# Issuing the V-cache transfers of a decode-attention kernel from the ACT queue instead of the SP queue

## The chip, the cores and the metric

The kernel runs on one core of a Trainium2 chip. The metric is device time in microseconds (us), taken from the profiled core; lower is better. The core has a TensorE (PE), a VectorE (DVE), a ScalarE (ACT), a GpSimd (POOL) and a SyncE (SP), each with its own instruction stream. Transfers from HBM to on-chip memory are run by 16 DMA engines. SP and ACT can each issue transfers; each has its own DMA ring (q1 and q10 in the profiles below), a list of transfers that the DMA engines work off.

All runs that are compared here are fast runs, and each experiment was timed beside the kernel before on the same chip. Repeats of a kernel agree within 0.3%.

## The reference, cut to what matters

Four layers of one-token attention, A, B, A, B. In each layer 32 heads read their own K and V cache.

```python
# per layer: x is one row of 640, 32 heads, 8192 cached positions, head size 192
q = layernorm(x) @ wq                       # 640 x 6144
scores = einsum("hd,hkd->hk", q, k_cache) * 192 ** -0.5
p = softmax(scores)
o = einsum("hk,hkd->hd", p, v_cache)
x = x + o.reshape(6144) @ wo                # 6144 x 640
```

One head's K, and one head's V, is 8192 x 192 in bf16: 3072 KB. The program reads 868 MB and computes little with it.

## The kernel before

VectorE computes the scores: it multiplies the K tile by q in place (6.56 us) and adds up along the head dimension in a tree. ACT makes the softmax weights, PE multiplies them with V. Three buffers hold K, three hold V. The kernel is written as one loop in which every engine appends to its own stream, so the place of a call in the loop sets the order within that engine's stream.

```python
def sp_k(h, Kt=Kt):
    i = counters["k"] % NKSLOT                  # 3 slots
    counters["k"] += 1
    SP.wait(T["kslot"][i])                      # the row maximum of head h-3 is done
    ...                                         # dma_start(kslot[i], K[h])
    return i, SP.op(f, sem=semK[i], inc=16)

def sp_v(h, Vt=Vt):
    i = counters["v"] % NVSLOT                  # 3 slots
    counters["v"] += 1
    SP.wait(T["vslot"][i])                      # PE is done with V of head h-3
    ...                                         # dma_start(vslot[i], V[h])
    return i, SP.op(f, sem=semV[i], inc=16)
...
# start of a layer (l > 0)
for npair in range(min(NWQSET, NPAIR)):
    ev_wq[npair] = sp_wq(npair)
need_k(0); need_k(1); need_v(0); need_k(2)
ev_wo[0] = sp_wo(0)
...
for h in range(HRUN):                           # 32 heads
    need_k(h); need_k(h + 1); ...; need_v(h)    # SP: K(h+1), then V(h)
    ...
    cur = stage_tree_a(h, ki, ev_k)             # DVE: multiply
    if h >= 1: stage_M(heads[h - 1])
    if h >= 2: stage_out_dve(heads[h - 2])
    stage_tree_a2(cur)
    if h >= 1: stage_softmax(heads[h - 1], ...) # ACT: softmax; PE: times V(h-1)
    stage_act_rows(cur)                         # ACT: 8 of the 64 score columns
    if h >= 2: stage_out(heads[h - 2])          # ACT and PE: output row times wo
    stage_tree_b(cur)                           # DVE: rest of the tree; ACT: copy of the maximum
... # the last head's softmax and output, then the next layer
```

SP does nothing but issue. It runs ahead of the loop until a buffer is not yet free. ACT issues nothing.

Of the kernel before, what the change touches and what calls it, by code (L numbers as in the profile page):

```python
# [115 lines left out]
def build(nc, A_x, A_k, A_v, A_wq, A_wo, B_x, B_k, B_v, B_wq, B_wo, out, dbg=None, cfg=None):  # L116
# [34 lines left out]
    with ExitStack() as ctx:  # L151
        def sb(name, shape, dt):
            return ctx.enter_context(nc.sbuf_tensor(name, shape, dt))
# [4 lines left out]
        def sem(name):  # L158
            return ctx.enter_context(nc.semaphore(name))

        kslot = [sb(f"kslot{i}", [128, JJ * DH], BF16) for i in range(NKSLOT)]
        vslot = [sb(f"vslot{i}", [128, JJ * DH], BF16) for i in range(NVSLOT)]
# [46 lines left out]
        semV = [sem(f"semV{i}") for i in range(NVSLOT)]  # L209
# [6 lines left out]
        SP = Stream("SP", None)  # L216
        PE = Stream("PE", pPE)
        DV = Stream("DVE", pDVE)
        AC = Stream("ACT", pACT)
# [33 lines left out]
        for i_ in range(2):  # L253
# [5 lines left out]
        T = dict(  # L259
            kslot=[None] * NKSLOT,  # L260
            vslot=[None] * NVSLOT,
            wq=[None] * 2,
            wo=[None] * 2,
            qb=[None, None],
            qslot=[None] * 8,
            sa=[None, None],
            ob=[None, None],
# [16 lines left out]
        for l in range(NL):  # L284
# [30 lines left out]
            def sp_v(h, Vt=Vt):  # L315
                i = counters["v"] % NVSLOT
                counters["v"] += 1
                SP.wait(T["vslot"][i])
                def f(s, i=i, h=h):
                    return s.dma_start(vslot[i][:, :], Vt[0, h].rearrange("(p j) d -> p (j d)", p=128))  # L320
                return i, SP.op(f, sem=semV[i], inc=16)

            ev_wq = [None] * NPAIR
            ev_wo = [None] * NG
# [8 lines left out]
            def need_v(h):  # L333
                if h >= H:
                    return
                if ("v", h) not in kv:
                    kv[("v", h)] = sp_v(h)
# [428 lines left out]
```

## Time and profile before

| | |
|---|---|
| time | 2074.65 us median of 2 runs (2075.35 to 2075.65 us in the medians of the later sets of 9) |
| K and V transfers | 256 of 3072 KB, one landing every 7.3 us |
| VectorE work per head | 13.7 us |
| VectorE waiting for K | 213 us, in 105 of 128 heads |

From the page of the kernel before: the mean busy share of the 16 DMA engines in 40 slices of the span (9 is 90% or more), what they moved in each slice, the DMA ring, the engines' shares of the chain of work that ended last, VectorE's multiply (count, busy us, mean ns, idle us just before it), and two of the DMA issues (size of one, median us from issue to landing).

```profile
DMA  9999999999999999999999999999999999999995
GB/s 395 430 425 428 422 422 427 426 430 419 423 426 425 427 422 424 426 426 428 418 423 426 423 429 424 422 427 426 426 410 425 425 423 424 423 423 425 426 427 254
...
q1 hardware_dynamic: 77700, 868.24, 99.3%
...
DMA 45%; issue 25%; DVE 24%; PE 4%; ACT 1%; SPq 1%; POOL 0%; POOLq 0%; DVEq 0%; ACTq 0%
...
L463 DVE TENSOR_TENSOR kslot<-kslot,q_sb 128x12288 bf16<-128x12288 bf16 x128 | 839.3, 6557 | 226.2 <-DMA kslot<-in_A_k_cache_dram 116.6
...
kslot<-in_A_k_cache_dram SPq DMA_DIRECT2D x64, 3072.0 KB, 32.6
vslot<-in_A_v_cache_dram SPq DMA_DIRECT2D x64, 3072.0 KB, 36.1
```

The DMA engines are busy throughout, on one ring, at 410 to 430 GB/s in all slices but the first and the last. Most of the chain of waits is DMA. VectorE works 13.7 us per head, a K and a V take 14.6 us, the weights 1.2 us more on average: DMA is the limit, by 2 us per head.

From the waits of the kernel before: who waited for what, us in total, times, longest.

```profile
DVE kslot L463 <- DMA kslot<-in_A_k_cache_dram: 116.6, 56, 8.2
DVE kslot L463 <- DMA kslot<-in_B_k_cache_dram: 96.6, 49, 6.8
...
PE OB L557 <- DMA vslot<-in_B_v_cache_dram: 4.4, 5, 0.9
```

VectorE waits for K. PE hardly waits for V: V is early, K is just in time.

From the timeline of SP: start, us, instruction. Each pair is K(h+1), then V(h).

```profile
906.95 2.21 SPq L312 DMA_DIRECT2D kslot<-in_B_k_cache_dram  x1
909.30 6.51 SPq L320 DMA_DIRECT2D vslot<-in_B_v_cache_dram  x1
921.56 0.33 SPq L312 DMA_DIRECT2D kslot<-in_B_k_cache_dram  x1
923.45 3.78 SPq L320 DMA_DIRECT2D vslot<-in_B_v_cache_dram  x1
```

K goes out as soon as VectorE has finished a head, V 2 us later. An issue takes 0.33 us, or several us when many transfers are queued (median 0.33 us with four in flight, 3.8 us with six). On this one ring what is issued first lands first. In layer 0 the landing records of the trace (when a transfer's completion was signalled) give:

```
transfer   issued   landed
K(31)      469.9    503.0
V(30)      475.2    510.3
V(31)      486.5    517.8
```

So when the last K of a layer lands, two V transfers are still to come. The stretch that follows is the only one in which VectorE stands still for long: it finishes the last head (13.7 us), then waits 22 to 23 us for the softmax, the output product, the layer norm and the next q. The windows view for that stretch, from the landing of K(31) to the end of head 0 of the next layer (the last two numbers are the DMA share and GB/s):

```profile
core 0: us, PE busy (x) PEld busy (x) DVE busy (x) ACT busy (x) POOL busy (x), PEclk, DMA share, GB/s
503.00:553.50 50.50, 23.60 (x186) 16.65 (x184) 31.59 (x29) 12.05 (x60) 0.54 (x1) 0.71 1.00 417
```

DMA stays busy through it: V(30), V(31), the weights and the first K and V of the next layer are queued.

### The profile page before, as it was taken

What the parts mean: (1) busy time and instruction counts of PE and PEld (TensorE: products, weight loads), DVE (VectorE), ACT (ScalarE), POOL (GpSimd) and SP (SyncE); (2) the same over time, 40 slices, a digit from 0 to 9 for tenths busy, and PEclk for the clock granted to TensorE, in tenths of its full rate; (3) what the DMA queues carried; (4) which work ended last, traced back from release to release, by engine and by line L of the source; (5) the groups of instructions that cost most, each with busy time, mean ns of one, the idle gap of its engine ahead of it and who ended that gap; (6) DMA issues with size and microseconds to landing.
All of it is one profiled execution on the core that took longest, in us unless ns stands there. A gap on an engine that the chain in (4) does not pass through costs nothing.

```text
span 2073.2 us, 24389 instructions
## 1 busy us (share of the span) xinstructions
PE 1158.3 (56%) x9625; PEld 915.1 (44%) x9668; DVE 1764.8 (85%) x1190; ACT 596.1 (29%) x3254; POOL 3.1 (0%) x13
## 2 busy tenths in 40 slices
PE   2565556555465555566536565556563665556656
PEld 1444444444354444444425454445452454444444
DVE  7888888988698888898779888889878988888896
ACT  2222232232232322232223332223222332223232
POOL 0000000000000000000000000000000000000000
PEclk7777777877678777777767777777776777777877
DMA  9999999999999999999999999999999999999995
GB/s 395 430 425 428 422 422 427 426 430 419 423 426 425 427 422 424 426 426 428 418 423 426 423 429 424 422 427 426 426 410 425 425 423 424 423 423 425 426 427 254
DMA packets 77813, 869.79 MB, mean 420 GB/s; under 512 B 4994, under 2 KB 29572, under 8 KB 44932
## 3 DMA queue, kind: packets, MB, share of 16 engines
q1 hardware_dynamic: 77700, 868.24, 99.3%
q8 instruction: 76, 1.25, 0.2%
q14 instruction: 37, 0.30, 0.0%
HBM read 868.22 MB, written 0.00 MB: 419 GB/s over the span
## 4 chain that ended last, share of the span: by engine, by line
DMA 45%; issue 25%; DVE 24%; PE 4%; ACT 1%; SPq 1%; POOL 0%; POOLq 0%; DVEq 0%; ACTq 0%
DMA kslot<-in_B_k_cache_dram 28%; DMA kslot<-in_A_k_cache_dram 17%; DVE kslot L463 12%; DVE kslot L504 5%; DVE kslot L492 4%; PE OB L557 3%; DVE s_sb L508 1%; SPq L312 0%; DVE M_sb L530 0%; DVE m_sb L515 0%; PE QB L412 0%; PE YL L632 0%; ACT p_sb L547 0%; DVE rl_sb L572 0%; SPq L295 0%
## 5 line engine op out<-in xcount | busy, mean ns | idle before, releaser
L463 DVE TENSOR_TENSOR kslot<-kslot,q_sb 128x12288 bf16<-128x12288 bf16 x128 | 839.3, 6557 | 226.2 <-DMA kslot<-in_A_k_cache_dram 116.6
L557 PE MATMUL OB<-vslot,p_sb 128*1 128x192 bf16 x8192 | 951.1, 294 | 84.3 <-ACT p_sb L547 78.6
L557 PEld LDWEIGHTS OB<-vslot,p_sb 128*1 128x1 bf16 x8192 | 809.6, 101 | 205.7 <-ACT p_sb L547 93.5
L539 PE MATMUL SA<-M_bf,ones_bf 1*128 1x1 bf16 x128 | 22.9, 179 | 689.2 <-ACT M_bf L537 689.2
L504 DVE TENSOR_TENSOR kslot<-kslot 128x2688 bf16<-128x2688 bf16 (+2 forms) x384 | 374.4, 975 | 13.3
L492 DVE TENSOR_TENSOR kslot<-kslot 128x5376 bf16<-128x5376 bf16 x128 | 374.7, 2927 | 0.1
L481 ACT ACTIVATE kslot<-kslot 128x192 bf16<-128x192 bf16 x1024 | 355.3, 348 | 22.2 <-DVE kslot L463 22.2
L539 PEld LDWEIGHTS SA<-M_bf,ones_bf 1*128 1x128 bf16 x128 | 12.4, 97 | 725.0 <-ACT M_bf L537 725.0
L537 ACT ACTIVATE M_bf<-M_sb 1x1 bf16<-1x1 f32 x128 | 26.5, 207 | 666.3 <-DVE M_sb L530 666.3
L481 ACT ACTIVATION_READ_ACCUMULATOR kslot<-kslot 128x1 f32 x1024 | 192.1, 188 | 0.0
L508 DVE TENSOR_REDUCE s_sb<-kslot 128x56 f32<-128x672 bf16 x128 | 109.1, 852 | 4.4
L632 PE MATMUL YL<-wo,oT_sb 128*1 128x512 bf16 x256 | 83.0, 378 | 51.8 <-ACT oT_sb L609 31.7
L605 ACT ACTIVATE oT_sb<-OB 128x1 bf16<-128x1 f32 x64 | 11.2, 175 | 310.9 <-PE OB L593 310.9
L608 ACT ACTIVATE oT_sb<-OB 64x1 bf16<-64x1 f32 x64 | 10.9, 170 | 281.0 <-PE OB L597 281.0
L412 PE MATMUL QB<-wq,xT_b 128*128 128x512 bf16 x197 | 57.5, 426 | 11.2 <-issue 6.4
L523 PE MATMUL SA<-ident,m_bf 128*1 128x128 bf16 x128 | 28.2, 221 | 54.5 <-ACT m_bf L520 54.5
L632 PEld LDWEIGHTS YL<-wo,oT_sb 128*1 128x1 bf16 x256 | 20.7, 81 | 79.7 <-ACT oT_sb L609 37.2
L634 PE MATMUL YH<-wo,oT_sb 128*1 128x128 bf16 x256 | 55.9, 218 | 0.0
L425 ACT ACTIVATE q_sb<-QB 128x512 bf16<-128x512 f32 x48 | 28.7, 598 | 93.6 <-PE QB L412 93.6
L578 ACT ACTIVATE orow_bf<-OB,rl_sb 1x192 bf16<-1x192 f32 x128 | 51.0, 399 | 1.7 <-DVE rl_sb L572 1.7
L547 ACT ACTIVATE p_sb<-s_sb,negm_sb 128x64 bf16<-128x64 f32 x128 | 44.8, 350 | 4.1
L530 DVE TENSOR_REDUCE M_sb<-SA 1x1 f32<-1x128 f32 x128 | 34.7, 271 | 12.6 <-PE SA L523 12.6
(50 smaller groups left out, 368.9 us busy)
## 6 DMA issues: line engine op xcount, KB each, us to landing
kslot<-in_A_k_cache_dram SPq DMA_DIRECT2D x64, 3072.0 KB, 32.6
vslot<-in_A_v_cache_dram SPq DMA_DIRECT2D x64, 3072.0 KB, 36.1
kslot<-in_B_k_cache_dram SPq DMA_DIRECT2D x64, 3072.0 KB, 32.6
vslot<-in_B_v_cache_dram SPq DMA_DIRECT2D x64, 3072.0 KB, 36.3
wq<-in_A_wq_dram SPq DMA_DIRECT2D x12, 1280.0 KB, 24.9
wo<-in_A_wo_dram SPq DMA_DIRECT2D x16, 960.0 KB, 38.2
wq<-in_B_wq_dram SPq DMA_DIRECT2D x12, 1280.0 KB, 25.7
wo<-in_B_wo_dram SPq DMA_DIRECT2D x16, 960.0 KB, 38.6
```

What stands on the lines that cost most here:

```text
L412: return t.matmul(QB[nb % 2][:, 0:ncols], lhsT=xT_b[:, c, :], rhs=wq_buf[s_][:, c, (nb % 2) * 512:(nb % 2) * 512 + ncols], start=(c == 0), ...
L463: e = DV.op(lambda v, k3=k3, qb_ap=qb_ap: v.tensor_tensor(k3, k3, qb_ap, ALU.mult))
L481: ea = AC.op(lambda a, k3=k3, par=par, j=j: a.activation(k3[:, j, :], k3[:, j, :], ACT.Copy, accum_out=s_sb[par][:, j:j + 1]))
L492: e = DV.op(lambda v, kt=kt, hw_=hw_: v.tensor_tensor(kt[:, :, 0:hw_], kt[:, :, 0:hw_], kt[:, :, hw_:DH], ALU.add))
L504: e = DV.op(lambda v, kt=kt, hw_=hw_, w=w: v.tensor_tensor(kt[:, :, 0:hw_], kt[:, :, 0:hw_], kt[:, :, hw_:w], ALU.add))
L508: cur["s"] = DV.op(lambda v, kt=kt, par=par, w=w, JA=JA: v.tensor_reduce(s_sb[par][:, JA:JJ], kt[:, :, 0:w], AX.X, ALU.add))
L539: cur["negM"] = PE.op(lambda t, par=par: t.matmul(SA[par][:, SA_NEGM:SA_NEGM + 1], lhsT=ones_bf[0:1, 0:128], rhs=M_bf[par][0:1, 0:1], star ...
L547: cur["p"] = AC.op(lambda a, par=par: a.activation(p_sb[par][:], s_sb[par][:], ACT.Exp, bias=negm_sb[par][:], scale=C))
L557: return t.matmul(OB[par][0:1, 0:DH], lhsT=p_sb[par][:, j:j + 1], rhs=vs3[:, j, :], start=(j == 0), stop=(j == JJ - 1))
L578: cur["orow"] = AC.op(lambda a, par=par: a.activation(orow_bf[par][:], OB[par][0:1, 0:DH], ACT.Copy, scale=rl_sb[par][0:1, 0:1]), tag=(f"O ...
L632: return t.matmul(YL[0:1, 0:512], lhsT=lhsT, rhs=rhs[:, 0:512], start=st, stop=sp_)
L634: return t.matmul(YH[0:1, 0:D - 512], lhsT=lhsT, rhs=rhs[:, 512:D], start=st, stop=sp_)
```

## The change

The intent is to have K and V go through two hardware rings, so that their issue and their traffic are independent.

```diff
             def sp_v(h, Vt=Vt):
                 i = counters["v"] % NVSLOT
                 counters["v"] += 1
-                SP.wait(T["vslot"][i])
+                AC.wait(T["vslot"][i])
                 ...
-                return i, SP.op(f, sem=semV[i], inc=16)
+                return i, AC.op(f, sem=semV[i], inc=16)
```

It does two things at once. V gets its own ring, and V's issue gets a place in ACT's program order. ACT does not run ahead as SP does, so V(h) goes out about one head later than before.

## The prediction

> **What bounds the kernel now.** The DMA engines. In the slices of the page they are at 9 tenths in 39 of 40 and move 420 to 430 GB/s; the chain of waits is 45% DMA landing of the K cache. One K or V transfer (3072 KB) lands about every 7.3 us, in order of issue, so a head costs DMA 14.6 us plus about 1.2 us of weights. VectorE needs 13.7 us per head (multiply 6.56, tree 2.93 + 2.99, reduce 0.85, max 0.22), and waits for K in 105 of 128 heads, 213 us in all (waits view).
>
> **What the change does not give.** The Trainium skill (DMA: Bandwidth & Descriptors, "Issuing engines are not separate DMA queues") says that SP and ACT queues run on the same 16 DMA engines and that a second one saves only issue time. This trace agrees that there is nothing more to win: one ring already delivers 3.15 MB per 7.3 us = 432 GB/s. SP's issues do block (0.33 us free, but up to 24 us where many weight descriptors are queued), yet five transfers are then in flight, so that time is not on the path.
>
> **What it moves.** The V issue now stands in ACT's program order, at the head of each iteration, behind ACT's output stage of an earlier head and its copy of the column maximum. On SP, V(h) went out about 2.4 us after VectorE finished head h-2; on ACT it goes out about 3 us after VectorE finished head h-1: one head later. Cost on ACT: 128 x 0.33 to 0.5 us = about 50 us, in idle time. V is shared with K by turns, so it takes about 15 us to land instead of 36, about 18 us after the end of head h-1; it is needed about 8 us after the end of head h, some 22 us. So in the middle of a layer PE waits little, VectorE still waits for K with another K queued behind it, and DMA stays full.
>
> **Where it costs.** (1) Three layer boundaries: VectorE stands still 23 us. Before, SP ran ahead and queued V(0), V(1) of the next layer; about 21 us of transfers were still waiting when head 0 ended. Now V(0) waits for ACT's last output stage (about 13 us after the last K head) and V(1) for head 0. Work queued from the landing of the last K: about 48 us, against 51 us until the next K is issued; and V(31) may land 2 us after it is wanted. I expect 3 to 6 us of DMA idleness each, about 12 in all. (2) The tail: before, V(30) and V(31) landed after the last K, 14.6 us hidden under VectorE's last head. Now only V(31) does, so the last K lands some 4 to 7 us later.
>
> Sum: +16 us: predicted 2090 us, range 2072 to 2112. Chances: faster by over 2% 0.02, within 2% 0.90, slower 0.08.
>
> **What would show it.** Two hardware rings of about equal K and V bytes; V latency 36 to about 16 us, K latency about unchanged or shorter; PE idle for V landing small in mid-layer; DMA digits 9 except near 515, 1030, 1550 us; last K landing later than 2043 us.
>
> **What would make it wrong.** ACT's issue blocking for several us and delaying its rows of the scores, which VectorE waits for (slower); two interleaved streams running at another rate than one (either way); V landing after PE wants it in every head, so that ACT, PE and the next V issue slip together (slower, over 2%).

## The result, and the profile after

The changed kernel takes 2097.61 us (median of 2 runs, 2096.88 and 2098.34), against 2074.65 us. The ratio is 1.011 (95% interval 1.0081 to 1.014), so the change is 1.1% slower. Ratios are the mean time of one kernel's fast runs over that of the other's of the same rounds, so not quite the ratio of the medians.

From the page of the changed kernel, the same parts:

```profile
DMA  9999999999899999999989999999998999999995
GB/s 397 426 427 425 425 419 427 427 427 423 369 428 424 427 420 424 425 427 424 424 369 424 426 428 420 423 427 425 427 425 363 425 424 425 425 424 427 424 428 229
...
q1 hardware_dynamic: 59268, 465.58, 53.4%
q10 hardware_dynamic: 18432, 402.66, 45.0%
...
DMA 38%; DVE 32%; issue 25%; PE 4%; ACT 1%; SPq 0%; POOL 0%; ACTq 0%; POOLq 0%; DVEq 0%
...
L463 DVE TENSOR_TENSOR kslot<-kslot,q_sb 128x12288 bf16<-128x12288 bf16 x128 | 838.8, 6553 | 244.6 <-DMA kslot<-in_A_k_cache_dram 127.3
...
kslot<-in_A_k_cache_dram SPq DMA_DIRECT2D x64, 3072.0 KB, 30.6
vslot<-in_A_v_cache_dram ACTq DMA_DIRECT2D x64, 3072.0 KB, 18.7
```

The bytes are split between rings q1 and q10. The rate drops in three slices, 369, 369 and 363 GB/s, at the three layer boundaries (423 to 425 in the same slices before), and in the last one, 229 instead of 254. In the others it is 419 to 428 as before, apart from the first. V now lands after 18.7 us instead of 36.1, K after 30.6 instead of 32.6. VectorE's idle time before the multiply rose by only 18 us. From the waits of the changed kernel:

```profile
DVE kslot L463 <- DMA kslot<-in_A_k_cache_dram: 127.3, 27, 15.6
DVE kslot L463 <- DMA kslot<-in_B_k_cache_dram: 104.5, 26, 14.6
...
PE OB L557 <- DMA vslot<-in_A_v_cache_dram: 3.5, 2, 2.6
...
PE OB L557 <- DMA vslot<-in_B_v_cache_dram: 2.1, 2, 1.3
```

VectorE waits half as often (53 times instead of 105) but somewhat longer in total (232 instead of 213 us), up to 15.6 us at once. PE still hardly waits for V, but two of its four waits, 2.6 us in layer 0 and 1.3 us in layer 1, fall into the boundary, where V(31) lands after PE wants it. VectorE's standstill there, from the end of head 31 to the first multiply of the next layer, is 26.1, 24.7 and 24.7 us long at the three boundaries, against 22.9, 22.1 and 23.1 us in the kernel before.

From ACT's timeline: the last ACT work of layer 0, then V(0) of the next layer; and 24 us later V(1), right after head 0.

```profile
537.75 0.17 ACT L608 ACTIVATE oT_sb<-OB 64x1 bf16<-64x1 f32 x1 [0.34 <-PE OB L597]
537.76 0.33 ACTq L320 DMA_DIRECT2D vslot<-in_B_v_cache_dram  x1
...
561.65 0.20 ACT L520 ACTIVATE m_bf<-m_sb 128x1 bf16<-128x1 f32 x1 [4.28 <-DVE m_sb L515]
561.66 0.35 ACTq L320 DMA_DIRECT2D vslot<-in_B_v_cache_dram  x1
```

From the view of the V tile: the number of issues on ACT, and the shortest, median and longest one in ns.

```profile
L320 ACTq DMA_DIRECT2D vslot<-in_A_v_cache_dram x64: 334/334/436, 2.1 to 1547.8; - x64
```

ACT is never held up by an issue. The windows view of the boundary (same columns as before), from the landing of K(31) to the end of head 0:

```profile
508.00:561.60 53.60, 25.33 (x189) 17.49 (x186) 31.61 (x29) 12.12 (x60) 0.54 (x1) 0.67 0.92 380
```

That is 380 GB/s where the kernel before moved 417. The landing records show why:

```
transfer   issued   landed
K(31)      477.2    508.0
V(29)      478.6    498.8
V(30)      492.6    510.4
V(31)      509.3    527.9
```

V(29) was issued after K(31) and landed 9 us before it. V(30) was issued 15 us after K(31) and landed 2.5 us after it. V overtakes K. At the end of head 0 (561.6 us) everything issued had landed, and no packet moved for 3.8 us, until the first of the next K.

To see where 21.8 us of the profiled spans (2095.0 against 2073.2 us) went, I added up from the DMA packets how far the rate fell short of 430 GB/s from the landing of each layer's last K until 6 us after head 0 of the next, and how much still moved after the program's last K:

| | before | after | cost |
|---|---|---|---|
| short of 430 GB/s, three boundaries | 1.4 + 1.9 + 2.8 us | 8.2 + 8.2 + 8.7 us | 19.0 us |
| moved after the program's last K | 3.89 MB | 3.24 MB | 0.65 MB / 430 GB/s = 1.5 us |
| last K landed to end | 29.7 us | 30.3 us | 0.6 us |
| sum | | | 21.1 of 21.8 us |

Inside layers (heads 8 to 26) both kernels move 424 GB/s. The loss is idle DMA at the boundaries, as the prediction said. What empties the rings there is the question for the experiments. There are two candidates: V is issued late, or V overtakes K.

### The profile page after: what moved, and what is told of

It is laid out like the page before. It is cut to its first block, busy times and chain, and to the rows that moved or that the text cites. A ratio compares the mean times of both kernels' runs of the same rounds, so it can differ in the third digit from the quotient of the medians.

```text
span 2095.0 us, 24432 instructions
## 1 busy us (share of the span) xinstructions
PE 1150.4 (55%) x9668; PEld 909.8 (43%) x9668; DVE 1760.3 (84%) x1190; ACT 600.7 (29%) x3254; POOL 3.1 (0%) x13
## 3 DMA queue, kind: packets, MB, share of 16 engines
q10 hardware_dynamic: 18432, 402.66, 45.0%
## 4 chain that ended last, share of the span: by engine, by line
DMA 38%; DVE 32%; issue 25%; PE 4%; ACT 1%; SPq 0%; POOL 0%; ACTq 0%; POOLq 0%; DVEq 0%
DMA kslot<-in_B_k_cache_dram 23%; DVE kslot L463 16%; DMA kslot<-in_A_k_cache_dram 14%; DVE kslot L504 6%; DVE kslot L492 6%; PE OB L557 3%; DVE s_sb L508 2%; DMA vslot<-in_B_v_cache_dram 1%; DMA vslot<-in_A_v_cache_dram 1%; DVE m_sb L515 0%; DVE M_sb L530 0%; PE QB L412 0%; PE YL L632 0%; DVE rl_sb L572 0%; ACT p_sb L547 0%
## 5 line engine op out<-in xcount | busy, mean ns | idle before, releaser
L557 PE MATMUL OB<-vslot,p_sb 128*1 128x192 bf16 x8192 | 936.1, 291 | 85.8 <-ACT p_sb L547 78.8
L412 PE MATMUL QB<-wq,xT_b 128*128 128x512 bf16 x240 | 67.4, 420 | 7.0 <-DMA wq<-in_A_wq_dram 4.3
L572 DVE RECIPROCAL rl_sb<-L_sb 1x1 f32<-1x1 f32 x128 | 18.1, 141 | 39.4 <-ACT junkL L568 39.4
## 6 DMA issues: line engine op xcount, KB each, us to landing
kslot<-in_A_k_cache_dram SPq DMA_DIRECT2D x64, 3072.0 KB, 30.6
vslot<-in_A_v_cache_dram ACTq DMA_DIRECT2D x64, 3072.0 KB, 18.7
```

Of the source, the lines that this page charges most:

```text
L412: return t.matmul(QB[nb % 2][:, 0:ncols], lhsT=xT_b[:, c, :], rhs=wq_buf[s_][:, c, (nb % 2) * 512:(nb % 2) * 512 + ncols], start=(c == 0), ...
L557: return t.matmul(OB[par][0:1, 0:DH], lhsT=p_sb[par][:, j:j + 1], rhs=vs3[:, j, :], start=(j == 0), stop=(j == JJ - 1))
```

## The experiments

### Ring and lateness, each by itself

Four runs on one chip. In the first, V stays on ACT but each call stands one head earlier, and the first two V of a layer go out at the boundary.

```diff
+                need_v(1)                      # at the start of a layer
...
                 need_k(h); need_k(h + 1); ...; need_v(h)
+                need_v(h + 1)
+                if h == H - 1 and l + 1 < NL:
+                    vpre[0] = sp_v(0, Vt=layers[l + 1]["v"])
```

> V stays on the ACT ring, but each V transfer is issued one head earlier in ACT's order (at the point where SP issued it in the kernel before), and the first two of the next layer before and right after the last ACT work of a layer. Theory (the lost time is the late issue, which leaves the DMA engines without work at the layer boundaries): 2068 to 2080 us, loss against 430 GB/s from the last K to the next K issue back from 6 us to 1 to 3 us per boundary, V landing after about 30 us or more. Rival (two rings sharing the engines by turns are slower, or hold K back): 2090 us or more, with the rate inside a layer at 423.5 GB/s as in the changed kernel instead of 425.

Measured: 2095.80 us against 2075.53 us, ratio 1.0102 (1.0088 to 1.0115). From its page, the slices and a K and a V issue:

```profile
GB/s 399 424 428 425 424 421 428 429 427 422 397 429 425 427 423 422 427 426 428 422 394 427 426 427 424 422 427 425 425 425 374 429 422 423 427 423 427 425 427 162
...
kslot<-in_A_k_cache_dram SPq DMA_DIRECT2D x64, 3072.0 KB, 30.8
vslot<-in_A_v_cache_dram ACTq DMA_DIRECT2D x64, 3072.0 KB, 19.0
```

The early issue brings almost nothing. V still lands after 19 us. The boundary loss is smaller (4.5 + 5.1 + 7.3 us), but now every V has landed when the program's last K lands: 0.0 MB moves after it, against 3.9 MB, which costs 9.1 us in the tail.

In the second, V is back on SP, but waits for the point in ACT's program at which the changed kernel issues it.

```diff
                 SP.wait(T["vslot"][i])
+                SP.wait((AC.sem, AC.counts[id(AC.sem)]))
...
-                need_k(0); need_k(1); need_v(0); need_k(2)
+                need_k(0); need_k(1); need_k(2)
                 ev_wo[0] = sp_wo(0)
+                need_v(0)
```

> V is back on the SP ring, but each V issue waits for the same point in ACT's program at which the changed kernel issues it (only the semaphore wait; in the boundary V(0) moves behind K(2) and the weights so that it holds none of them up). Theory: still slow, 2088 to 2105 us, with 5 to 7 us lost at each boundary. Rival (the second ring): 2070 to 2080 us.

Measured: 2076.11 us, ratio 1.0004 (0.9991 to 1.0016). From its page, the slices and a K and a V issue:

```profile
GB/s 395 430 426 427 423 422 427 427 428 415 417 426 426 427 423 422 427 426 429 416 409 425 423 429 423 423 426 426 427 416 419 425 423 428 425 422 427 426 426 269
...
kslot<-in_A_k_cache_dram SPq DMA_DIRECT2D x64, 3072.0 KB, 30.1
vslot<-in_A_v_cache_dram SPq DMA_DIRECT2D x64, 3072.0 KB, 22.9
```

V is as late as in the changed kernel, its time to landing falls to 22.9 us, and nothing is lost. So the theory of the prediction, that the late issue costs the time, fell in both runs: late issue on one ring is free, and early issue on two rings costs 20 us.

The third and fourth run undo the lateness in one place each: only at the boundary (the two additions for V(0) and V(1)), or only inside the layers (the line `need_v(h + 1)`).

> Two rings, V late inside a layer as in the changed kernel; only V(0) and V(1) of the next layer are issued early. Theory: the boundaries hold 14 of the 22 us lost, so 2081 to 2087 us, with at most 3 us lost per boundary, and the rate inside a layer stays near 423.5 GB/s.

Measured: 2097.27 us, ratio 1.0100 (1.0085 to 1.0116): no gain, and outside its range. Its windows view, for the boundary, the 18 us after head 0, and the layer:

```profile
509.30:562.00 52.70, 23.53 (x183) 16.47 (x181) 31.55 (x29) 12.12 (x60) 0.54 (x1) 0.66 1.01 421
562.00:580.00 18.00, 8.21 (x68) 6.79 (x68) 17.83 (x10) 4.21 (x23) 0.00 (x0) 0.65 0.74 288
580.00:1000.00 420.00, 240.61 (x2024) 192.07 (x2034) 370.32 (x247) 124.92 (x685) 0.00 (x0) 0.76 1.01 426
```

The boundary itself is repaired (421 GB/s). The idle time has moved to the next 18 us (288 GB/s, against 426 in the 18 us after head 0 in the kernel before): V(1) had landed already, so only one K was issued when head 0 ended, and it had landed by 574.1 us, before head 1 ended. A transfer that was moved forward is missing later.

> Two rings, V early inside a layer, but V(0) of a layer still behind the last ACT work of the layer before, and V(1) at head 0. Theory: most of the 6 us lost inside layers comes back if late issue causes it, while the boundaries keep a loss: V(1) goes out about 13 us before the next K (after the projected q is copied), so a part of the idle time goes too: 2078 to 2090 us. If the rate inside layers stays at 423.5 GB/s, the two rings cause that part.

Measured: 2097.05 us, ratio 1.0106 (1.0092 to 1.0120): no gain, and outside its range too, like the first and the third.

### A new theory: order

What the four runs leave is the second ring itself. Two readings are possible. Either two rings together move fewer bytes per us (call it R), or they change the order of arrival (O). The Trainium skill, page "DMA: Bandwidth & Descriptors", section "Queues, rings and completion order", says that each DMA engine takes turns between the rings it has work for. This trace agrees: from 562.5 to 578 us of the changed kernel, with one K and one V in flight, the two rings moved 204 and 198 GB/s, and the two transfers took 17.2 and 17.4 us to land; a K with no V in flight, right after head 0 in the third run, took 12.0, 11.2 and 10.6 us at the three boundaries. The K ring holds two K and the weights, the V ring one or two V. With equal turns the one on the shorter ring overtakes, even if it was issued later, as V(29) overtook K(31) above. R is already weak, since the rate inside layers did not change.

The next run takes V(30) and V(31) of each layer back to the SP ring, behind K(31); the rest is the changed kernel.

```diff
-                AC.wait(T["vslot"][i])
+                Q = SP if h >= H - 2 else AC
+                Q.wait(T["vslot"][i])
```

> The changed kernel, but V(30) and V(31) of each layer go through the SP ring, behind K(31), as in the kernel before; the other 30 of each layer stay on the ACT ring. New theory (O, order: the rings are served by turns, so a V that is issued late overtakes K and weights that were issued earlier; when the last K of a layer lands nearly all V has landed too, and too little is left to keep the DMA engines busy while VectorE stands still at the boundary and in the tail): 2076 to 2084 us; loss from the last K to the end of head 0 of the next layer from 8 us to 3 or less. Rival (R, two rings together move fewer bytes per us): the rate inside layers counts, so 2088 us or more.

Measured: 2086.84 us, ratio 1.0055 (1.0042 to 1.0067). Half of the loss is gone, which is less than O expected and more than R did. On SP these two V also go out earlier (V(30) of layer 0 at 477.0 instead of 492.6 us, V(31) at 490.9 instead of 509.3), so this run changes order and lateness together.

The same on top of the first experiment:

> As the first experiment (two rings, V issued one head early), but V(30) and V(31) of each layer through the SP ring behind K(31). O: 2073 to 2080 us, with 3.5 MB or more moved after the last K of the program instead of 0. R: 2085 us or more.

Measured: 2084.11 us, ratio 1.0041 (1.0027 to 1.0055). Again better, again not enough. This pair of runs separates the ring from the lateness: in layer 0 V(30) and V(31) go out at 484.4 and 498.3 us here, at 484.5 and 498.1 us in the first experiment, and K(31) at 483.3 us in both. What differs is their ring, and K(31) lands at 502.6 instead of 515.9 us. The boundary loss is back to 2.0 + 1.8 + 1.5 us, and 5.3 MB move after the last K. But the last K now lands 37.3 us before the end instead of 29.7: it came while VectorE was still busy with earlier heads, because now V(29) had overtaken K(30) (in the last layer V(29) was issued at 2013.5 us and landed at 2027.0, K(30) was issued at 2011.5 and landed at 2037.0; in the kernel before K(30) landed at 2028.8). The delay had moved one head forward, where VectorE has too little slack to make it up.

The third run makes the order wrong on a single ring: V(30) and V(31) are issued just before K(31). Nothing else is changed in the kernel before.

```diff
+                if h == H - 2:
+                    need_v(h); need_v(h + 1)
                 need_k(h); need_k(h + 1); ...; need_v(h)
```

> The kernel before, all on the SP ring, with one swap: V(30) and V(31) of each layer are issued just before K(31), so that a single ring serves them first. O: the loss appears without a second ring: the tail alone costs 3.9 MB / 430 GB/s = 9 us, the boundaries 1 to 4 us each: 2084 to 2096 us, nothing moved after the last K. R: 2074 to 2078 us, since there is one ring.

Measured: 2101.58 us, ratio 1.0127 (1.0113 to 1.0141). From its page, the slices and the data ring:

```profile
GB/s 400 424 427 428 422 422 427 426 429 421 377 428 424 428 423 426 424 427 426 424 387 425 423 423 431 423 426 425 427 425 375 426 424 423 429 426 425 427 426 143
...
q1 hardware_dynamic: 77700, 868.24, 98.1%
```

There is one data ring, and the slices show the loss of the changed kernel: three dips at the boundaries (377, 387, 375), and a last slice of 143 GB/s. The loss is even larger than expected. Two V, 14.6 us, now stand in front of the last K, and in layer 0 K(31) lands exactly that much later (517.6 instead of 503.0 us). SP also issues K(31) 17 us later here (486.9 instead of 469.9 us), since it waits for V(31)'s buffer first; but transfers were queued all the while, V(31) landing 7.3 us before K(31), so K(31)'s place in the ring set its landing. My expectation had 9 us for the tail and 1 to 4 us for each boundary; by the packets the boundaries lost 5.6, 4.2 and 4.5 us more than before. This run shows that order alone can cost what the change cost, without a second ring.

The fourth run was to have two rings with the right order, by cutting every K and V in two halves, one for each ring.

```diff
-                SP.wait(T["kslot"][i])
-                ... s.dma_start(kslot[i][:, :], ...)
+                for Q, sm, a in ((SP, semK, 0), (AC, semKa, HF)):
+                    Q.wait(T["kslot"][i])
+                    evs.append(Q.op(lambda s, ...: s.dma_start(kslot[i][:, a:a + HF], src[:, a:a + HF]), sem=sm[i], inc=16))
# the same for V; issues of ACT moved one head forward to keep the lead of SP
```

> Each K and each V transfer is cut in two halves along the row; one half goes through SP, the other through ACT, in the same order K, V, K, V on both, with the lead of the kernel before. Two rings are always busy together, but their order agrees with the order of need. O: 2070 to 2082 us. R: 2090 us or more. (The packets are 12 KB instead of 24 KB; a small cost of that would stand in both.)

Measured: 2113.97 us, ratio 1.0188 (1.0174 to 1.0202), 32 us above what O expected and in the range of R. Its slices and its K issues:

```profile
GB/s 396 422 423 419 420 421 423 422 422 422 358 424 422 419 420 421 423 422 422 421 380 424 421 421 421 421 421 424 421 418 376 423 422 422 419 420 422 423 424 210
...
kslot<-in_A_k_cache_dram SPq DMA_DIRECT2D x64, 1536.0 KB, 30.9
kslot<-in_A_k_cache_dram ACTq DMA_DIRECT2D x64, 1536.0 KB, 11.8
```

The design did not do what it was meant for. ACT's half of K lands after 11.8 us, SP's half after 30.9, so ACT's ring runs ahead, and VectorE needs both halves. SP's ring carries the weights as well, which is the likely reason. The rate is also lower in most slices. The control for this is below.

### Swapping the rings, and a dose

If O is right, the sign of the effect depends on who overtakes. So K alone goes to the ACT ring (two heads ahead in ACT's order), and V and the weights stay on SP.

```diff
-                SP.wait(T["kslot"][i])
+                AC.wait(T["kslot"][i])
...
-                return i, SP.op(f, sem=semK[i], inc=16)
+                return i, AC.op(f, sem=semK[i], inc=16)
...
+                if h + 2 < H:
+                    need_k(h + 2)
+                elif l + 1 < NL:
+                    pre[h + 2 - H] = sp_k(h + 2 - H, Kt=layers[l + 1]["k"])
```

> The rings are swapped: K alone on the ACT ring (issued two heads ahead in ACT's order, the first two of the next layer ahead of the boundary), V and all weights on the SP ring. Two rings are as busy together as in the changed kernel. O (what is issued late on the emptier ring overtakes; harm comes only when V overtakes K): now K overtakes V, so the last K of layer 0 lands before 503 us, more than one V is in flight when it lands, and the time is 2064 to 2080 us. R (two rings cost, whatever they carry): 2088 us or more.

Measured: 2077.76 us, ratio 1.0010 (0.9997 to 1.0022). The DMA view shows its K and V issues, the waits view who waited for data:

```profile
kslot<-in_A_k_cache_dram ACTq DMA_DIRECT2D x64, 3072.0 KB, 19.5
vslot<-in_A_v_cache_dram SPq DMA_DIRECT2D x64, 3072.0 KB, 36.7
```

Who waited, us in total, times, longest:

```profile
PE OB L558 <- DMA vslot<-in_A_v_cache_dram: 196.3, 24, 18.1
...
PE OB L558 <- DMA vslot<-in_B_v_cache_dram: 150.5, 20, 18.6
...
DVE kslot L464 <- DMA kslot<-in_A_k_cache_dram: 8.3, 1, 8.3
```

Two rings are as busy as in the changed kernel (402.66 MB on ACT's ring in both), and the loss is gone. Now K lands after 19.5 us and V after 36.7. VectorE waits for K once, PE waits for V 347 us. In layer 0 the last K lands at 495.9 us, 7 us sooner than before, and three V are still to come. It is not faster than the kernel before: the tail now hangs on V(31), which lands at 2058.8 us as before (2058.0).

The dose: of the 32 V of a layer the last eight go through SP, behind their K, instead of the last two (`h >= H - 8` in place of `h >= H - 2`).

> As the run with V(30) and V(31) on the SP ring (2084 us), but with V(24) to V(31) of each layer there; 24 of 32 V per layer stay on the ACT ring. O: with two the overtaking was only moved to V(29) and K(30), 7 us that VectorE cannot make up in the last head; with eight heads it can make up 1 to 2 us in each: 2073 to 2079 us. R, or a cost per V on the ACT ring: 2082 us or more.

Measured: 2075.84 us, ratio 1.0004 (0.9990 to 1.0017). With 0, 2 and 8 of the last V on SP the times are 2095.8, 2084.1 and 2075.8 us. Three quarters of all V still go through the ACT ring, and the loss is gone. So V on ACT's ring costs nothing in the middle of a layer. It costs where the stream of K ends.

The control for the halves: both on the SP ring.

> Control for the run with halves on both rings (2114 us, 420.5 GB/s inside layers): the same halves, both on the SP ring, in the order of the kernel before. If the smaller packets cost the rate: 420 to 421 GB/s and 2088 to 2096 us, so that some 20 us of the 38 were packets and the rest was one ring running ahead of the other. If the second ring costs the rate: 424 GB/s and 2074 to 2078 us.

Measured: 2093.86 us, ratio 1.0089 (1.0075 to 1.0102), and 420 GB/s inside layers.

So 18 of the 38 us were the cut itself, with one ring. Whether it is the shorter rows (12 KB) or the doubled number of transfers is not separated. That the other 20 us came from one ring running ahead is what the landing times suggest; no run takes it away by itself.

### A fix that was none

The last run moves the weights to ACT as well, so that K is alone on SP.

```diff
-    build(nc, ..., out)
+    build(nc, ..., out,
+          cfg=dict(wq_on_act=True, wo_on_act=True))
```

> The changed kernel, with the weights too on the ACT ring, so that K is alone on the SP ring and V, still issued late, stands behind the weights. O: K now has the emptier ring and the weights no longer stand in front of it, so it is overtaken by less: the last K of layer 0 lands before 508 us, and the time falls to 2074 to 2088 us, though V is as late as in the changed kernel or later. R, or the theory of the prediction (the late issue of V): 2092 us or more. If ACT is held up by its issues (the weights have 5 to 6 times as many packets), ACT's share of the chain of waits rises and the time with it; that would show apart from both.

Measured: 2132.83 us, ratio 1.0280 (1.0266 to 1.0294), the slowest of all, and far outside what O expected; by its time alone it would speak for R or for lateness. As O says, the last K of layer 0 lands sooner (506.0 against 508.0 us), K takes 18.6 us to land, and VectorE never waits for K. But its slices on the page are:

```profile
GB/s 352 427 428 424 422 427 424 429 425 426 280 428 425 425 422 426 424 430 426 425 283 425 424 428 422 423 427 428 420 428 285 428 423 427 423 422 426 426 427 251
```

Here the boundaries fall to 280, 283 and 285 GB/s. SP's timeline shows four K issues in one stretch, the last of them at its end, at 575.3 us; ACT's timeline shows when the weights of the next layer went out. SP's:

```profile
501.25 74.41 SPq L312 DMA_DIRECT2D kslot<-in_B_k_cache_dram  x4
```

And ACT's:

```profile
551.45 0.39 ACTq L295 DMA_DIRECT2D wq<-in_B_wq_dram  x1
...
551.87 0.54 ACTq L295 DMA_DIRECT2D wq<-in_B_wq_dram  x1
552.44 0.55 ACTq L320 DMA_DIRECT2D vslot<-in_B_v_cache_dram  x1
553.01 0.54 ACTq L304 DMA_DIRECT2D wo<-in_B_wo_dram  x1
```

The weights for the next q stand behind ACT's last output work, 21 us after VectorE had finished the layer (530.2 us). The next layer cannot start without them, and when they went out nothing else was in flight: the three K had landed. VectorE's standstill grew to 30 to 31 us, and the DMA engines fell 18 to 19 us short of 430 GB/s at each boundary, counted as in the table above (1 to 3 us in the kernel before). Here a late issue does cost, because what is late is what everything waits for. How much of the shortfall is the weights and how much the V behind them, no run separates. PE also waits for V all along, 451 us in total by the waits view.

My expectation had looked at the rings only and had overlooked that place in ACT's order.

## Why the prediction was right or wrong

The time was right: 2090 us predicted, 2097.6 measured, inside 2072 to 2112, and slower by about 1%. That the sum came out near is partly luck: one of its two terms was too small and the other too large.

- **DMA is the limit and a second ring adds no rate: right.** Both kernels move 424 GB/s inside layers. The sentence of the Trainium skill ("DMA: Bandwidth & Descriptors", section "Issuing engines are not separate DMA queues"), that a second issuer only saves issue time, agrees as far as rate goes.
- **Issue on ACT costs ACT nothing: right.** 0.33 us each, at most 0.44, ACT at 29% as before.
- **V lands after about 16 us, PE does not wait: right** (18.7 us; 5.6 us of waiting in total). The prediction also named the exception, V(31) landing 2 us after it is wanted: 2.6 us in layer 0.
- **Boundaries, "3 to 6 us of DMA idleness each, about 12 in all": too small.** The runs show 19.0 us.
- **Tail, "some 4 to 7 us": too large.** 1.5 us in bytes and 0.6 us in the end. The prediction left only V(31) to land after the program's last K; V(30) landed after it too (2066.5 against 2064.7 us).
- **The cause given for the boundaries failed.** The step reads: "Now V(0) waits for ACT's last output stage ... and V(1) for head 0." Late issue on one ring costs 0.04%, early issue on two rings 1.02%, and V(0) and V(1) issued early bring no gain. What the runs show instead is the order: V(29) to V(31), on the shorter ring, overtake K and the weights, so that too little is left to move while VectorE stands still. V before K on one ring costs 1.27%, and with the last eight V of a layer back behind their K, three quarters of V still on ACT's ring, the cost is gone. The prediction knew that V is "shared with K by turns" and landed in half the time, and drew the consequence, a later last K, for the tail alone. For the boundaries it did not ask what lands later when V lands sooner.

What stays open: how the loss of the changed kernel divides between lateness and order at the boundary itself. With early issue the boundaries lose 16.9 instead of 25.1 us, and the tail takes 7 of these 8 us back. Both numbers come from traces of one run each. Part of the 25.1 us falls into the 1.6 to 3.2 us by which VectorE's standstill is longer, V(31) being late. A longer standstill alone need not cost: with the last eight V on SP it is 25.8 to 29.1 us, and nothing is lost, because enough is queued.

## What to carry to other kernels

In these runs, with DMA as the limit, one ring was a schedule: K and V landed in the order of issue (K(31), V(30), V(31) issued at 469.9, 475.2, 486.5 us and landed at 503.0, 510.3, 517.8), and the program wrote that order. A second ring replaced it with turns (204 and 198 GB/s), and the shorter ring won, whatever was more urgent. Before you split a stream, ask which stream the critical engine waits for, what overtakes it, and what is left to move in the stretch where that engine stands still.

## What the Trainium skill lacked or had wrong

- "DMA: Bandwidth & Descriptors", sections "Issuing engines are not separate DMA queues" and "Rules for kernel authors": spreading transfers over issuers is said not to help, and to save issue time only. It is not said that it can harm. Here the order of arrival changed and the kernel lost 1.1%; a wrong order on a single ring lost 1.3%.
- The same page, "Queues, rings and completion order": turns between rings are described, but not what they do to a transfer: with two streams of 24 KB rows each ring moved half (204 and 198 GB/s), and a 3072 KB transfer took 17 us to land, where one with no second stream beside it took 10.6 to 12.0.
- The same page, "Rules for kernel authors": the row "Max bandwidth" asks for 128 partitions and at least 1 MiB per DMA. That is not contradicted here, but above it size still counted a little: cutting 3072 KB transfers (24 KB rows) into 1536 KB ones (12 KB rows) on one ring cost 0.9%, 420 instead of 424 GB/s inside layers.
- No page says what it costs to issue a transfer from an engine that has other work: the issue waits for its place among ACT's instructions, and SP's running ahead is lost. For V that lateness alone cost nothing on one ring (ratio 1.0004). With the weights on ACT as well, the weights went out 21 us after VectorE had finished the layer, and the time was 2.8% longer.
